# Unnormalised exponentials in the first four stages of an attention and feed-forward kernel, and float16 pairs for half of its first float32 units

## The chip, the cores and the metric

The kernel runs on one core of one Trainium2 chip. The metric is the device time of one execution in microseconds (us). The kernel before took 642.29 us (median of three runs: 640.42, 642.29 and 642.66).

## The reference

Attention over q, k and v of shape (4, 8, 768, 64), with a window of 16 around each query and 24 block summaries as extra keys, then a feed-forward layer on the 3072 tokens of 512 numbers (w_in is 512 x 2048, w_out 2048 x 512):

```python
k_sum = k.reshape(B, H, nb, block, D).max(axis=3)
v_sum = v.reshape(B, H, nb, block, D).mean(axis=3)
scores_l_m = np.where(np.abs(pos[:, None] - pos[None, :]) < window, scale * q @ k.T, -1e9)
scores_s = scale * np.einsum('bhsd,bhnd->bhsn', q, k_sum) + np.log(block)
scores_all = np.concatenate([scores_l_m, scores_s], axis=-1)
a = np.exp(scores_all - scores_all.max(axis=-1, keepdims=True))
a = a / (a.sum(axis=-1, keepdims=True) + 1e-09)
x = a @ np.concatenate([v, v_sum], axis=2)          # (token, head * 64 + d)
h = x @ w_in
out = (h * (1.0 / (1.0 + np.exp(-h)))) @ w_out
```

The weights arrive as float64, everything else as float32; the output is float32.

## The kernel before, in words

**Tiling.** Attention is cut into 24 stages of 128 queries (stage s is tile s mod 6 of batch s // 6), each of four jobs m = 4s + g of two heads. A query tile sees 158 local keys and 24 summaries, 182 columns. A job (`job_a`) computes its scores on PE (L587 in batch 0, in float32 on 64 rows of the array; L589 and L590 with split operands later) into a PSUM bank, takes the masked row maximum on DVE (L594), the exponential with its row sum on ACT (L597), and the sum's reciprocal on DVE (L602, L603). In a "plain" stage (s < NPL, before: stages 0 and 1) the exponentials are scaled by the reciprocal (L612 or L608), transposed on PE (L621, L623: a "turn") and copied back to SBUF in two halves; `job_c` multiplies them with float32 v at once (L653). In the other stages they are scaled into float16 p (L608, L610, L612), the rounding remainder is made on DVE (L636, four instructions for a job), a DMA transposes both (L639), and `job_c` multiplies with float16 pairs of v (L668, 40 matmuls for a stage). `job_x` takes the stage's result from bank 7 into the float16 pair xh, xl (L222 on ACT, L229 on DVE).

**Feed-forward.** Two stages make a chunk of 256 tokens; 12 chunks of 8 units (f = 0 to 7, 256 of the 2048 columns) are 96 units. A unit is 24 matmuls 128x256 of FFN1 (L781: xh and xl with the pair of w_in), a tanh on ACT (L795), the product on DVE (L796), and FFN2 (L790). Chunks 0 and 1 (c < NPW) use float32 in FFN2, 4 matmuls 128x512 that the trace shows as 8 records (4 for each half of the tokens); the others use a float16 pair of g and of w_out, 12 matmuls 128x512 (6 for each half). The order of the units is (chunk 0, f 0 to 3), (1, f 0 to 3), (1, f 4 to 7), (0, f 4 to 7), then chunk after chunk.

**Weights.** w arrives as float64 in 16 tiles of 1 MB, loaded by SP. ACT (L704, L700) and DVE (L702, L706) turn each into float32. w_in tiles are then reduced (L716), gathered on PE (L720, L721), and split into a pair (L222 on ACT, L229 on DVE). w_out tiles are summed on ACT (L714) and split only after one scale `kap` over all of them is known (`job_wo`).

**Order.** All engines run in program order. That order is written by a planner (class `Plan`) that knows a cost in ns for every step and a priority from the table `TUNE`; it also puts fills (L321, matmuls into bank 0 that compute nothing) on PE where it expects PE to wait before the first unit.

Of the kernel before, what the change touches and what calls it, by code (L numbers as in the profile page):

```python
# [9 lines left out]
F32 = mybir.dt.float32  # L10
# [4 lines left out]
AF = mybir.ActivationFunctionType  # L15
# [33 lines left out]
NPL = 2  # L49
# [158 lines left out]
def local_attn_ffn(ctx: ExitStack, tc: tile.TileContext, qkT, qF, qD, kF, kD, v, vR, w, out):  # L208
# [100 lines left out]
    e_t = ring(NE, [P, 2, NKEY], F32, "e")  # L309
    p_all = const.tile([P, NP * 2 * UW], F16, name="p")  # L310
# [4 lines left out]
    part_t = [const.tile([P, 2, DM], F32, name=f"part{i}") for i in range(NSUP - 2)]  # L315
# [251 lines left out]
    def job_a(m, prio):  # L567
# [9 lines left out]
        k = (2, 3, 4, 5)[m % 4] if m < 8 else sbank()  # L577
        sc = bank[k].rearrange("p (a b) -> p a b", a=2)
        n = m % NE
        tt, ttk = tt_of(m)  # L580
        et, mx, pt = e_t[n], mx_t[n], p_t[m % NP]
        pr = slice(g % 2 * 64, g % 2 * 64 + 64)
# [18 lines left out]
        unit_sum = 1.0 if s < NPL else 1.0 / PSC
        plan.op({"dve": 72}, lambda e: nc.vector.tensor_scalar(out=su, in0=su, scalar1=1e-9, scalar2=unit_sum, op0=ALU.add, op1=ALU.mult), w=sums, prio=prio)  # L602
        plan.op({"dve": 75}, lambda e: nc.vector.reciprocal(out=su, in_=su), w=sums, prio=prio)  # L603

        def scaled(e, out, i):
            by = su[:, i:i + 1]
            if e == "act":
                nc.scalar.activation(out=out, in_=et[:, i, :], func=AF.Copy, scale=by)  # L608
            elif e == "pool":
                nc.gpsimd.tensor_scalar(out=out, in0=et[:, i, :], scalar1=by, scalar2=0.0, op0=ALU.mult, op1=ALU.add)  # L610
            else:
                nc.vector.tensor_scalar(out=out, in0=et[:, i, :], scalar1=by, scalar2=None, op0=ALU.mult)  # L612
# [28 lines left out]
    def job_c(m, prio):  # L641
# [15 lines left out]
        if g < 3:  # L657
            return
# [300 lines left out]
```

## Time and profile before

| | us |
|---|---|
| median of three runs | 642.29 |
| profiled execution | 642.86 |
| its span in the profile | 641.1 |
| PE busy | 629.0 (98%) |
| DVE busy | 467.8 (73%) |
| ACT busy | 407.6 (64%) |
| POOL busy | 178.9 (28%) |
| first matmul of the first unit | 52.30 |
| first matmul of unit 8 | 105.16 |
| first matmul of unit 16 | 165.02 |

The profiled execution is 1.76 us longer than its span and 0.57 us above the median. A row of the trace gives a start, a duration, engine, line, operation, what is written and read, and how many alike instructions in a row it holds; PE's rows include the tail of the last matmul, so the next row can start before one ends. The chain of waits gives times from one start to the next instead.

### The profile page before, as it was taken

Reading aid. Unit: us, or ns where it says so; the run is one execution under the profiler, and the core shown is the slowest. Engines: PE = TensorE matmul, PEld = TensorE weight load, DVE = VectorE, ACT = ScalarE, POOL = GpSimd, SP = SyncE. Lnnn points to the kernel's source line nnn. Section 1 sums busy time; section 2 is a strip of 40 time slices with the busy share of each in tenths; the row PEclk is TensorE's granted clock in tenths of the full one; section 3 lists DMA queues with packets and bytes.
Section 4 is the critical chain, followed back from the end, with each engine's and each line's share of the span. In section 5 each row is a group of like instructions: output and inputs, shape, how many; then the busy total and the mean of one; then the engine's idle time right before and its main releaser. Section 6 shows DMA issues by size and latency. Waiting matters only on the chain.

```text
span 641.1 us, 13605 instructions
## 1 busy us (share of the span) xinstructions
PE 629.0 (98%) x4940; PEld 425.8 (66%) x4940; DVE 467.8 (73%) x1365; ACT 407.6 (64%) x895; POOL 178.9 (28%) x200
## 2 busy tenths in 40 slices
PE   7999999999999999999999999999999998999997
PEld 2667666656676776667677676666776675767664
DVE  6999886899779954897779855899898984231322
ACT  3899897964677655765778655656887863332322
POOL 3035232110564222242534245024542330000000
PEclk9999999999999999999999999999999999999999
DMA  8869986365485665665484774566686551000000
GB/s 308 308 195 304 295 341 179 98 192 138 131 191 122 135 187 194 144 170 137 122 198 121 175 225 127 141 174 118 196 179 153 113 129 32 35 0 1 34 1 33
DMA packets 99237, 97.37 MB, mean 152 GB/s; under 512 B 76886, under 2 KB 79958, under 8 KB 97122
## 3 DMA queue, kind: packets, MB, share of 16 engines
q1 hardware_dynamic: 99170, 96.51, 54.7%
q8 instruction: 38, 0.62, 0.4%
q14 instruction: 29, 0.24, 0.1%
HBM read 70.34 MB, written 6.29 MB: 120 GB/s over the span
## 4 chain that ended last, share of the span: by engine, by line
PE 65%; DVE 12%; ACT 8%; DMA 8%; issue 3%; SPq 2%; POOL 2%; POOLq 0%; DVEq 0%; ACTq 0%
PE bank L790 29%; PE bank L781 27%; DVE p L636 4%; DMA raw<-in_v_dram 2%; PE bank L668 2%; PE bank L587 2%; DVE qk L494 2%; DMA raw<-vms 2%; DMA raw<-in_kD_dram 2%; ACT wt L704 2%; DVE e L594 1%; PE bank L589 1%; PE bank L590 1%; PE bank L522 1%; DMA wt<-in_w_dram 1%
## 5 line engine op out<-in xcount | busy, mean ns | idle before, releaser
L790 PE MATMUL bank<-wt,g 128*128 128x512 f16 (+1 forms) x1088 | 283.2, 405 | 3.1 <-ACT g L800 1.1
L781 PE MATMUL bank<-xh,wt 128*128 128x256 f16 x1536 | 269.6, 273 | 0.0
L781 PEld LDWEIGHTS <-wt 128*128 128x128 f16 x2304 | 224.1, 98 | 43.0 <-issue 5.0
L781 PE MATMUL bank<-xl,wt 128*128 128x256 f16 x768 | 209.3, 273 | 0.0
L790 PEld LDWEIGHTS <-g 128*128 128x128 f16 x960 | 91.9, 98 | 96.2 <-DVE g L232 1.6
L796 DVE SCALAR_TENSOR_TENSOR t<-t,bank 128x512 f32<-128x512 f32 x96 | 65.6, 683 | 75.6 <-ACT t L795 75.2
L795 ACT ACTIVATE t<-bank,asc 128x512 f32<-128x512 f32 x96 | 65.2, 680 | 74.0 <-PE bank L781 73.5
L597 ACT ACTIVATE e<-e,mx 128x182 f32<-128x182 f32 x192 | 83.9, 439 | 35.9 <-DVE mx L594 32.9
L636 DVE SCALAR_TENSOR_TENSOR p<-e,sum,p 128x128 f16<-128x128 f32 x352 | 100.9, 349 | 7.9 <-ACT p L608 5.8
L232 POOL TENSOR_TENSOR g<-t,g 128x512 f16<-128x512 f32 x41 | 53.0, 1293 | 101.8 <-ACT g L800 101.7
L610 POOL TENSOR_SCALAR p<-e,sum 128x182 f16<-128x182 f32 x72 | 40.4, 567 | 142.1 <-DVE sum L603 42.1
L800 ACT CAST g<-t 128x512 f16<-128x512 f32 x80 | 49.2, 615 | 41.6 <-DVE t L796 40.4
L594 DVE CUSTOM_DVE_ANT_0 e<-bank,masks,qsc 128x182 f32<-128x182 f32 x144 | 52.7, 401 | 12.4 <-PE bank L590 12.1
L232 DVE TENSOR_TENSOR g<-t,g 128x512 f16<-128x512 f32 x39 | 32.8, 840 | 21.2 <-ACT g L800 21.1
L608 ACT ACTIVATE p<-e,sum 128x182 f16<-128x182 f32 x89 | 36.4, 439 | 13.8 <-DVE sum L603 5.2
L232 POOL TENSOR_TENSOR vv<-raw,vv 128x1024 f16<-128x1024 f32 x18 | 40.4, 2247 | 8.0 <-ACT vv L214 4.9
L790 PEld LDWEIGHTS bank<-wt,g 128*128 128x128 f32 x128 | 22.5, 190 | 23.2 <-issue 20.3
L597 ACT ACTIVATION_READ_ACCUMULATOR e<-e,mx 128x1 f32 x192 | 36.3, 189 | 0.0
L494 DVE SCALAR_TENSOR_TENSOR qk<-raw,qsc,qk 64x1264 f16<-64x1264 f32 x18 | 28.9, 1608 | 1.6 <-ACT qk L493 1.0
L668 PEld LDWEIGHTS <-vv 128*64 128x64 f16 x880 | 25.2, 110 | 6.8 <-issue 6.4
L493 ACT ACTIVATE qk<-raw,qsc 128x1264 f16<-128x1264 f32 x18 | 24.2, 1344 | 6.9 <-DMA raw<-in_kD_dram 6.9
L589 PE MATMUL bank<-qk 128*128 128x182 f16 x144 | 27.7, 242 | 0.0
(153 smaller groups left out, 656.3 us busy)
## 6 DMA issues: line engine op xcount, KB each, us to landing
wt<-in_w_dram SPq DMA_DIRECT2D x16, 1024.0 KB
raw<-in_kD_dram SPq DMA_DIRECT2D x18, 632.0 KB
raw<-in_v_dram SPq DMA_DIRECT2D x20, 512.0 KB
raw<-in_qD_dram SPq DMA_DIRECT2D x18, 512.0 KB
out_dram<-raw SPq DMA_DIRECT2D x24, 256.0 KB
raw<-in_kF_dram SPq DMA_DIRECT2D x12, 384.0 KB
raw<-in_qF_dram SPq DMA_DIRECT2D x9, 512.0 KB
raw<-in_vR_dram SPq DMA_DIRECT2D x12, 384.0 KB
```

Source lines behind the costliest of these rows:

```text
L232: eng[e].tensor_tensor(out=out, in0=in0, in1=in1, op=ALU.subtract)
L494: plan.op({"dve": 1450}, lambda e: nc.vector.scalar_tensor_tensor(out=kst[64:, :, :NLOC], in0=kr[64:], scalar=qs[64:, 1:2], in1=kst[64:, : ...
L594: plan.op({"dve": 258 if b == 0 else 323}, lambda e, i=i: nc.vector.tensor_tensor_reduce(out=et[:, i, :], in0=sc[:, i, :NKEY], in1=mask, s ...
L597: plan.op({"act": 431}, lambda e, i=i, h=h: nc.scalar.activation(out=et[:, i, :], in_=et[:, i, :], func=AF.Exp, scale=-1.0, bias=mx[:, i:i ...
L610: nc.gpsimd.tensor_scalar(out=out, in0=et[:, i, :], scalar1=by, scalar2=0.0, op0=ALU.mult, op1=ALU.add)
L636: nc.vector.scalar_tensor_tensor(out=pt[:, i, to:to + z - a], in0=et[:, i, a:z], scalar=su[:, i:i + 1], in1=pt[:, i, a:z], op0=ALU.mult, o ...
L668: nc.tensor.matmul(out=av[j * D:(j + 1) * D, i * P:(i + 1) * P], lhsT=vt[:, vi, h * D:(h + 1) * D], rhs=tt[:, j * 3 + blk, :], start=(n == ...
L781: nc.tensor.matmul(out=h[:, d * CH:(d + 1) * CH], lhsT=wt[f, 0][:, part, d, ct * P:(ct + 1) * P], rhs=x[:, ct, :], start=(ct == 0 and q == ...
L790: nc.tensor.matmul(out=bank[ob[u]], lhsT=a[:, d * CH + u * P:d * CH + u * P + P], rhs=b[:, d, :], start=(opens and d == 0 and q == 0), sto ...
L795: plan.op({"act": 640}, lambda e: nc.scalar.activation(out=t, in_=h, func=AF.Tanh, scale=asc_t[c // 3 % 2][:, f:f + 1]), r=[("bank", k), ( ...
L796: plan.op({"dve": 605}, lambda e: nc.vector.scalar_tensor_tensor(out=t, in0=t, scalar=1.0, in1=h, op0=ALU.add, op1=ALU.mult), r=[("bank", ...
L800: plan.op({"act": 540}, lambda e: nc.scalar.copy(out=gh, in_=t), r=[("t", j)], w=[("gh", n)], prio=at - TUNE["post"])
```

## The change: what it does

- `NPL` goes from 2 to 4: stages 0 to 3 are plain. In them the exponentials are not scaled. Their sums are collected in a tile `ss` of 128x8 for a stage; `job_x` inverts it, spreads it over 64 rows with eight float32 matmuls (`over`, L691 of the new kernel) into bank 1, 1, 5 or 4, scales that (`xr`), multiplies bank 7 with it on DVE (L695), casts to xh on ACT (L697) and makes xl on POOL or DVE.
- In batch 0 the scores of two jobs are issued together, alternating between rows 0 to 63 and 64 to 127 of the array and between banks k and k + 1.
- A turn is copied back at once, 512 columns, instead of in two halves; banks 2 to 5 are cleared at the start for that.
- The product with v of a plain stage is issued once a stage, 16 matmuls (L657), and not once a job.
- Units f = 4 to 7 of chunks 0 and 1 use the float16 pair in FFN2. Their banks close after f = 3, the partial result is scaled and kept, and is added at the end. So `kap` and the first pairs of w_out are needed by unit 8 instead of unit 16.
- All numbers of `TUNE` are other ones, and with them the order on every engine; some costs of the planner too.

```diff
-NPL = 2
+NPL = 4
+    for i in range(2, 6):
+        nc.vector.memset(bank[i], 0.0)
...
-        k = (2, 3, 4, 5)[m % 4] if m < 8 else sbank()
+        k = (2, 3, 4, 5)[m % 4] if m < 8 else (4, 5)[m % 2] if m < 16 else (6, 7)[m % 2] if b == 0 else sbank()
...
-                    nc.tensor.matmul(out=sc[:, i, :NKEY], lhsT=qk[pr, hp, :P], rhs=qk[pr, hp, P:], start=True, stop=True)
+                    for o in range(2):
+                        pr = slice(o * 64, o * 64 + 64)
+                        nc.tensor.matmul(out=bank[k + o][:, i * 256:i * 256 + NKEY], lhsT=qk[pr, hp, :P], rhs=qk[pr, hp, P:], start=True, stop=True)
...
-                out=et[:, i, :], in_=et[:, i, :], func=AF.Exp, scale=-1.0, bias=mx[:, i:i + 1], accum_out=su[:, i:i + 1]),
+                out=et[:, i, :NKEY], in_=et[:, i, :NKEY], func=AF.Exp, scale=-1.0, bias=mx[:, i:i + 1], accum_out=ss_t[s % 2][:, 2 * g + i:2 * g + i + 1] if plain else su[:, i:i + 1]),
...
-            for i in range(2):
-                plan.op({"dve": 190, "act": 310}, lambda e, i=i: scaled(e, et[:, i, :], i), r=sums, w=[("e", n, i)], prio=prio)
...
-            plan.op({"act": 264, "dve": 335}, lambda e: copy(e, tt[:, :2, :], tp[:, :2, :]), r=[("bank", k)], w=[ttk], prio=prio, port=())
-            plan.op({"act": 264, "dve": 335}, lambda e: copy(e, tt[:NS2, 2:, :], tp[:NS2, 2:, :]), r=[("bank", k)], w=[ttk + ("side",)], prio=prio, port=())
+            plan.op({"act": 530, "dve": 600}, lambda e: copy(e, tt, tp), r=[("bank", k)], w=[ttk], prio=prio, port=())
...
+            rb = (1, 1, 5, 4)[s]
+            def over(e):
+                for h in range(H):
+                    g, j = divmod(h, 2)
+                    nc.tensor.matmul(out=bank[rb][j * D:(j + 1) * D, g * P:(g + 1) * P], lhsT=ss[:, h:h + 1].to_broadcast([P, D]), rhs=ident, start=True, stop=True)
+            plan.op({"act": 600, "dve": 600}, lambda e: times(e, xr, bank[rb], vsc_t[0][:, 0:1]), r=[("bank", rb), ("vsc", 0)], w=[("xr", s % 2)], prio=prio, port=())
+            plan.op({"dve": 620}, lambda e: nc.vector.tensor_tensor(out=xr, in0=bank[k], in1=xr, op=ALU.mult), r=[("bank", k)], w=[("xr", s % 2)], prio=prio, port=())
+            plan.op({"act": 560}, lambda e: nc.scalar.copy(out=xh, in_=xr3), r=[("xr", s % 2)], w=[("xh", z, half)], prio=prio)
+            plan.op({"dve": 680, "pool": 1280}, lambda e: less(e, xl, xr3, xh), r=[("xr", s % 2), ("xh", z, half)], w=[("xl", z, half)], prio=prio)
...
-        plain = c < NPW
+        plain = c < NPW and f < QF
-        split = c < NSUP - 2
+        split = c < NSUP
...
-    job_wo(need_c[NPW] - TUNE["kap"])
+    job_wo(need_f[QF] - TUNE["kap"])
```

**PE ahead of the first unit.** In the kernel before, all sixteen jobs' scores and the whole of stages 0 and 1 stand ahead of the first L781 (bank_195 is bank 0, bank_201 bank 6, bank_202 bank 7); the last rows ahead of it, and the first row of it:

```order
L587 MATMUL bank_201<-qk_152 128x182 x2
...
L653 MATMUL bank_202<-wt 64x128 x4
L587 MATMUL bank_201<-qk_152 128x182 x2
L653 MATMUL bank_202<-wt 64x128 x12
L587 MATMUL bank_201<-qk_152 128x182 x2
...
L720 MATMUL bank_201<-wm,spread 128x2
L721 MATMUL bank_201<-least,spread 128x2
...
L668 MATMUL bank_202<-wt,vv_166 64x128
...
L781 MATMUL bank_195<-xh_186,wt 128x256
```

In the new kernel (bank_199 is bank 0, bank_206 bank 7), lines 591, 611 and 613, 657, 691 and 801 are scores, turns, the product with v, `over` and FFN1:

```order
L591 MATMUL bank_203<-qk_152 128x182
L591 MATMUL bank_204<-qk_152 128x182
...
L691 MATMUL bank_200<-ident,ss_177 64x128 x8
L657 MATMUL bank_206<-wt 64x128 x16
L611 MATMUL bank_203<-ident,e_174 128x128 x2
L613 MATMUL bank_203<-ident,e_174 54x128 x2
...
L691 MATMUL bank_200<-ident,ss_178 64x128 x8
L657 MATMUL bank_206<-wt 64x128 x16
...
L801 MATMUL bank_199<-xh_190,wt 128x256
```

Of stages 2 and 3 only one joint score pair and one turn stand ahead of the first unit now; the float16 product L668 that stood there has gone, and 61 fills stand ahead of the first L801 instead of 105.

**PE between units 1 and 3 of the new kernel** (bank_203 and bank_204 are banks 4 and 5; L810 is FFN2):

```order
L810 MATMUL bank_201<-wt,g_196 128x512 x2
L691 MATMUL bank_204<-ident,ss_177 64x128 x8
L810 MATMUL bank_202<-wt,g_196 128x512 x2
...
L591 MATMUL bank_203<-qk_152 128x182
L591 MATMUL bank_204<-qk_152 128x182
...
L657 MATMUL bank_206<-wt 64x128 x16
L611 MATMUL bank_203<-ident,e_174 128x128 x2
```

In the kernel before, PE had at that place, beside L781 and L790, only the gathers and one L668 product. Seven turns, three score pairs, two `over` and two products with v, fourteen pieces of stages 2 and 3, now stand from unit 0 to ahead of unit 4.

**DVE ahead of the first unit.** Before, remainders of p and the operand xl of chunk 0:

```order
L636 SCALAR_TENSOR_TENSOR p<-e_174,sum_168,p 128x128
L636 SCALAR_TENSOR_TENSOR p<-e_174,sum_168,p 128x54
...
L716 TENSOR_REDUCE wm<-wt 128x1
...
L229 SCALAR_TENSOR_TENSOR xl_188<-bank_202,vsc_164,xh_186 128x4x128
```

Now (L736 is L716 of before, L684, L685 and L695 are new, L599 is L594 of before):

```order
L599 ISA e_175,mx_172<-bank_204,masks 128x182
...
L736 TENSOR_REDUCE wm<-wt 128x1
L695 TENSOR_TENSOR xr_179<-bank_206,xr_179 128x512
L684 TENSOR_SCALAR ss_178<-ss_178 128x8
...
L685 RECIPROCAL ss_178<-ss_178 128x8
...
L226 TENSOR_SCALAR xr_180<-bank_200,vsc_164 128x512
...
L695 TENSOR_TENSOR xr_180<-bank_206,xr_180 128x512
```

The twenty remainders are gone, and the operand's last step before ACT's cast is a product on DVE.

## Rows read from the trace of the kernel before

**Rows 1.** Windows: start:end, us, then busy us (instructions) of PE, PEld, DVE, ACT, POOL; clock, DMA share, GB/s.

```profile
11.20:49.30 38.10, 38.06 (x263) 24.58 (x262) 36.29 (x151) 33.08 (x99) 6.62 (x11) 1.00 0.83 265
52.30:105.20 52.90, 52.22 (x318) 33.13 (x315) 45.85 (x67) 47.89 (x67) 18.40 (x17) 1.00 0.86 294
105.20:165.00 59.80, 59.80 (x386) 38.00 (x385) 49.56 (x146) 41.06 (x85) 9.55 (x14) 1.00 0.52 145
```

**Rows 2.** Chain of waits, 145 to 167 and 560 to 570: start, us, what.

```profile
147.87 1.24 PE bank L668 x40
149.11 1.91 PE bank L790 x4
...
153.29 1.72 PE bank L790 x4
155.01 2.62 PE bank L781 x24
...
563.17 5.18 PE bank L790 x24
```

**Rows 3.** Chain of waits, start-up, PE.

```profile
9.56 1.52 PE bank L587 x8
11.08 1.53 PE bank L522 x2
...
14.25 0.97 PE bank L522 x2
15.22 0.81 PE bank L587 x4
...
17.00 0.37 PE bank L621 x2
17.37 0.22 PE bank L623 x2
```

**Rows 4.** Timeline of PE: start, us, instruction.

```profile
33.44 1.54 PE L653 MATMUL bank<-wt 128*64 128x128 f32 x16
```

**Rows 5.** DVE, 11.2 to 49.3, by form: count, busy us, mean ns, idle before.

```profile
L594 DVE CUSTOM_DVE_ANT_0 e<-bank,masks 128x182 f32<-128x182 f32 x32 | 10.0, 339 | 1.5 <-PE bank L587 1.5
L706 DVE SCALAR_TENSOR_TENSOR wt<-wt 128x1024 uint32<-128x1024 uint32 x4 | 4.9, 1217 | 0.1
L716 DVE TENSOR_REDUCE wm<-wt 128x1 f32<-128x1024 f32 x4 | 4.8, 1208 | 0.0
L636 DVE SCALAR_TENSOR_TENSOR p<-e,sum,p 128x128 f16<-128x128 f32 x10 | 3.6, 360 | 0.4 <-POOL p L610 0.4
L636 DVE SCALAR_TENSOR_TENSOR p<-e,sum,p 128x54 f16<-128x54 f32 x10 | 2.7, 265 | 0.0
L594 DVE DVE_READ_ACCUMULATOR2_ANT mx<- 128x1 f32 x32 | 2.6, 81 | 0.1
L612 DVE TENSOR_SCALAR e<-e,sum 128x182 f32<-128x182 f32 x9 | 2.5, 313 | 0.0
L602 DVE TENSOR_SCALAR sum<-sum 128x2 f32<-128x2 f32 x13 | 2.0, 156 | 0.0
...
L363 DVE TENSOR_REDUCE km<-wt 128x24 f32<-128x768 f32 x2 | 1.9, 950 | 0.0
L229 DVE SCALAR_TENSOR_TENSOR xl<-bank,vsc,xh 128x512 f16<-128x512 f32 x2 | 1.5, 736 | 0.0
```

**Rows 6.** ACT, the same stretch and columns.

```profile
L597 ACT ACTIVATE e<-e,mx 128x182 f32<-128x182 f32 x32 | 14.0, 441 | 6.2 <-DVE mx L594 4.9 <-DVE sum L603 0.9
```

**Rows 7.** Timeline of POOL, then DVE, around 50 us.

```profile
47.96 2.13 POOL L232 TENSOR_TENSOR vv<-wt,vv 128x1024 f16<-128x1024 f32 x1
...
49.49 1.69 DVE L229 SCALAR_TENSOR_TENSOR wt<-wt,ur 128x1024 f16<-128x1024 f32 x1
...
53.55 1.28 DVE L229 SCALAR_TENSOR_TENSOR wt<-wt,ur 128x1024 f16<-128x1024 f32 x1
```

**Rows 8.** Timeline of DVE: the last decoding of a weight tile.

```profile
95.31 1.97 DVE L706 SCALAR_TENSOR_TENSOR wt<-wt 128x1024 uint32<-128x1024 uint32 x1
```

More of the change, by code (lines that the diff above doesn't have):

```diff
@@ L590, in scores @@
                     nc.tensor.matmul(out=sc[:, i, :NKEY], lhsT=ql[:, h, :], rhs=kst[:, h, :], start=False, stop=True)
-        plan.op({"pe": 640 if b == 0 else 330}, scores, r=[(x, s % 2, hp) for x in ("qk", "qkm") for hp, _ in heads(g)] + [("qkk", s % 2)], w=[("bank", k)], prio=prio, cols=728)
+        if b or g % 2 == 0:
+            plan.op({"pe": 330 if b else 820}, scores, r=[(x, s % 2, hp) for x in ("qk", "qkm") for hp, _ in heads(g)] + [("qkk", s % 2)], w=[("bank", k)] if b else [("bank", k), ("bank", k + 1)], prio=prio, cols=728)
@@ L600, in job_a @@
+                w=[("e", n, i), ("ss", s % 2, 2 * g + i) if plain else ("sum", m % 3, i)], prio=prio)
         er, sums = [("e", n, 0), ("e", n, 1)], [("sum", m % 3, 0), ("sum", m % 3, 1)]
[L601 to L612, printed above, removed]
@@ L644, in job_c @@
         av = bank[7]
+        if g < 3:
+            return
         if s < NPL:
-            tt, ttk = tt_of(m)
             vr, key = plain_v[s]
+            parts = [tt_of(4 * s + i) for i in range(4)]
             def direct(e):
                 for blk in range(2):
-                    for j in range(2):
-                        rows = slice(0, P if blk == 0 else NS2)
-                        nc.tensor.matmul(out=av[j * D:(j + 1) * D, g * P:(g + 1) * P], lhsT=vr[rows, blk, (2 * g + j) * D:(2 * g + j + 1) * D], rhs=tt[rows, 2 * blk + j, :], start=(blk == 0), stop=(blk == 1))
-            plan.op({"pe": 850}, direct, r=[ttk, ttk + ("side",)] + key, w=[("bank", 7)], prio=prio, cols=728)
-            return
-        if g < 3:
+                    rows = slice(0, NS2 if blk else P)
+                    for i, (tt, _) in enumerate(parts):
+                        for j in range(2):
+                            nc.tensor.matmul(out=av[j * D:(j + 1) * D, i * P:(i + 1) * P], lhsT=vr[rows, blk, (2 * i + j) * D:(2 * i + j + 1) * D], rhs=tt[rows, 2 * blk + j, :], start=(blk == 0 and i == 0), stop=(blk == 1 and i == 3))
+            plan.op({"pe": 2100}, direct, r=[ttk for _, ttk in parts] + key, w=[("bank", 7)], prio=prio, cols=2912)
             return
@@ L808, in job_f @@
             src = bank[ob[u]]
+            pt = plain_w[c, 0][:, u, :] if split else None
             if f < NFP - 1:
-                pt = part_t[c][:, u, :]
-                plan.op({"act": 478, "dve": 598}, lambda e, pt=pt, src=src: copy(e, pt, src), r=[("bank", ob[u])], w=[("part", c, u)], prio=at - TUNE["post"])
+                plan.op({"act": 600, "dve": 600}, lambda e, pt=pt, src=src: times(e, pt, src, vsc_t[c // 3 % 2][:, 1:2]), r=[("bank", ob[u]), ("vsc", c // 3 % 2)], w=[("wv", c, 0)] if u == 0 else [("part", c)], prio=at - TUNE["post"], port=())
                 continue
@@ L839, in job_stage @@
             job_km(b, p[0] - TUNE["km"])
[L840 removed]
+        if s == NPL:
             for i in range(NP):
@@ L886, in local_attn_ffn @@
     plan.issue()
-TUNE = dict(wo=446.0, kap=120.96, km=193.98, w_dma=118.35, w_dec=-99.08, a0=174.58, a1=-468.24, d1=455.82, span=3.23, post=200.49, ffn2=-434.13, jc0=1039.26, jc1=-3.66, jx0=275.52, jx1=-673.16, vs=1070.72, qk=-145.44, k=-197.61, v=228.96, v0=83.48, out=338.89, first=69.59)
+TUNE = dict(wo=1435.66, kap=595.44, km=324.46, w_dma=-292.18, w_dec=-36.51, a0=618.19, a1=-173.71, d1=488.76, span=-168.31, post=-84.22, ffn2=-1333.64, jc0=2019.41, jc1=670.33, jx0=530.16, jx1=21.06, vs=2765.61, qk=-268.51, k=382.38, v=2035.94, v0=-52.65, out=942.25, first=210.86)
 NUDGE = {}
```

44 lines of the change are left out of this document (29 added, 15 removed).

## The prediction

> **What bounds the kernel now.** I read the windows first. From the first unit to the end PE is busy in nearly all of the time: 52.22 of 52.90 us in units 0 to 7, 59.80 of 59.80 in units 8 to 15 [rows 1]. There a us taken out of PE's queue is a us of time. Behind 165 us it is the same but for small gaps. The first 52.3 us are another matter: PE is full there too, but of fills, which take no part in the result. What sets the first unit is when its last operand, xl of chunk 0, leaves DVE. So I read DVE and ACT from the first score reduction (11.2) to that operand (49.3): DVE is busy in 36.29 of 38.10 us, ACT in 33.08 [rows 1]. DVE bounds that stretch, with ACT close behind: ACT's exponentials idle 6.2 us, 4.9 of them for DVE's maxima [rows 6].
>
> So three sums: the time of the first unit (52.3 before), from there to unit 16 (112.7 before: 52.90 + 59.80) [rows 1], and the rest (641.1 − 165.0 = 476.1).
>
> **Until the first unit.** DVE's groups of that stretch [rows 5], with fourteen smaller ones, add to 45.8 us. The engine is busy 36.29 because records overlap, so a group costs .79 of its busy sum. What leaves the stretch, read from the new order:
> - half of the 32 score reductions and of their accumulator reads, since stages 2 and 3 come later: 5.0 + 1.3;
> - all twenty remainders of p: 3.6 + 2.7;
> - nine scalings of exponentials: 2.5;
> - 22 of the 26 small sums and reciprocals (13 of each, alike): 3.4;
> - three of four weight reductions and two of four decodings, which move behind the first unit: 3.6 + 2.5;
> - the two key reductions, now ahead of the first scores, and the two operands xl from the bank, replaced below: 1.9 + 1.5.
>
> That is 28.0 us by busy sums, 22.1 of the engine's time. What enters: turns copied 512 wide (1.2 more for the halves that they replace, an estimate from the 512-wide xl at .74, [rows 5]), two products with bank 7 and one scaling of `xr` (at .66 each, .74 less the overlap, 2.0), one weight split moved forward (1.3 by [rows 7]), the two sums of `ss` (.3): 4.8. So 38.1 − 22.1 + 4.8 = 20.8. The first scores start about 11.9, as one key load now stands behind four loads of v on SP's queue (.7 later than 11.2). That gives 32.7; the cast on ACT and the remainder on POOL come behind it, 1.9 (half of POOL's 2.13 for half of its columns, [rows 7], and .8 for the cast, between .44 for 182 columns and three times that, [rows 6]): 34.6. I add 1.4 for waits between the engines, much less than ACT's 6.2 of before as DVE holds less that it waits for: the first unit starts at **36**. Without waits it is 33. If PE's start-up loses as much over its real work as before (10.7 us), it is 41. Of what leaves, remainders, scalings and small sums are never done again; the rest is done behind the first unit, under PE's work.
>
> **From unit 0 to unit 16, PE.** Start to start, one FFN1 takes 2.62, half a float32 FFN2 1.72 (1.91 behind a float16 product), a float16 FFN2 half of 5.18 [rows 2]:
> - 16 FFN1: 42.0.
> - 8 float32 FFN2 at 3.55 (two halves between 1.72 and 1.91): 28.4. Before, 15.5 of them took 55.0.
> - 7 float16 FFN2 at 2.59: 18.1. A unit is dearer in float32 by .96, so the eight changed ones give 7.7.
> - 7 joint score pairs. The single score of a job took .81; the first two jobs, issued next to one another on both halves of the array, 1.52 [rows 3]. That was with the array still slow: two matmuls L522 took 1.53 right behind, and .97 at 14.25 [rows 3], and the trace's first clock record (1.00) is at 12.2. I take half of 1.52, .76, for a pair, against two singles, 1.62: 5.3.
> - 7 turns at .59 [rows 3], less overlap: 3.7.
> - two `over`: eight matmuls 64 rows wide are as many records as sixteen of L653, 1.54 [rows 4]: 3.1. Two products with v of a whole stage, 32 records or twice 1.54 less overlap, 2.94 [rows 4]: 5.9.
> - two float16 products (stages 4 and 5) at 1.24 [rows 2]: 2.5; gathers and small matmuls: 2.8.
>
> Sum: 111.8. The same sum for before gives 110.3 against the measured 112.7, so 2.4 us are not in it (waits, and switches between shapes). I add these 2.4, and 3 for new waits between 0 and 5: PE now runs the fourteen pieces of stages 2 and 3 between units, and scores of stages 4 and 5 share bank 7 with the product with v. That is 117.2: **unit 16 starts at 153** instead of 165.0. Can DVE and ACT follow? DVE's busy time up to unit 16 falls by the remainders, scalings and sums of stages 2 and 3, but must be done by 153: before, 49.56 of 59.80 us went by in units 8 to 15 [rows 1]; by the new order I count 49 us of work in 52.6 there. It fits, barely, which is why I keep the waits.
>
> **From unit 16 to the end.** Nothing of the change is here but what slips behind: a float16 unit in place of a float32 one as the last leftover FFN2, and two more jobs' scores, +1.5. 476.1 + 1.5 = 477.6. Other edits cost nothing visible: the four memsets on DVE stand ahead of the first scores, where DVE waits for loads; the partial result's scaling and final addition run on ACT and DVE under FFN1, where DVE is idle 13 to 17% of the time and ACT 9 to 31% [rows 1]; if that cover were gone each costs about .7 us once for four banks.
>
> **Sum.** 36 + 117.2 + 477.6 = 630.8 of span, and 1.76 beside the span as in the profiled execution: 632.6, say **632.5**. The profiled execution (642.86) is .57 above the median, which the rounding of my terms covers.
>
> **One rule against it.** The remainder xl of stages 0 to 3 goes to POOL now, four times, with DVE at weight splits beside it. In the trace the split that met a POOL subtraction took 1.69 instead of 1.28, with .60 us of overlap [rows 7]: .41 each, 1.6 for four, inside my 3 us of waits.
> The Trainium skill (SBUF — State Buffer, "SBUF: two separate sides") says that the pair of ports which DVE with two SBUF inputs shares with GpSimd is an exclusive lock, so that the later one waits for the whole instruction. The trace agrees in kind: the split ended late by two thirds of the overlap. By that rule the four would cost DVE up to four whole POOL subtractions, some 4.3 by half of the POOL row's 2.13, and the sum would be 635 where DVE has no slack.
>
> **The rivals.**
> - *The scale comes late* (15 in 100). FFN2 of unit 8 now waits for `kap`, and so for the last decoded weight tile; DVE finished that one at 97.3 [rows 8], and kap, the first split and its signals took some 5 more at their shortest. If the last load is no earlier than before, FFN2 of unit 8 can start at 102.8 where PE wants it at 100.4: +2.4, 635. Loads fill 86% of the DMA engines' time up to there [rows 1], which speaks for it; that the planner has to do them for unit 8 and starts the units 16 us earlier speaks for both. Each us later costs one: up to 642.
> - *Stages 2 and 3 stall PE between units* (11 in 100, the slower side). PE's queue is in order: a turn that is not ready holds FFN1 behind it. A pair needs, from its first matmul, .76, a reduction of .26 and two exponentials of .44 before its first turn, about 2.2 with signals, and about .9 more for its second; the order leaves one FFN1 (2.62) or less. One weight step of 1.2 to 1.3 on DVE or ACT ahead of it [rows 5, 7] uses the slack up and more. With one such step in front of each of the fourteen pieces, 14 × 1.2 = 16.8 in place of my 3: 646.3, slower. It decides at 1.15 us a piece. Against: in units 0 to 7 of before PE waited under 1 us though weights were decoded there all the time. With half of it: 638.
> - *The halves of the array do not run beside one another* (4 in 100). Then a pair costs 1.62: +.86 × 7 = 6, 638.6.
> - *The clock falls* (4 in 100). It was at its upper level (1.00) in every stretch from 12.2 us on [rows 1], with fills ahead of the first unit and PE never idle; the change takes 44 fills out, and puts waits between units. One unit at the lower level costs its own 6.2 again: 638.8, two 645. The Trainium skill (TensorE: Matmul & The Clock Gate, Part 1) says that an idle array falls back to half of its clock; no row of before shows it behind 12.2 us.
> - *It goes better* (5 in 100): first unit at 33, no new waits: 625 or less.
>
> **How the numbers follow.** The forecast (625 to 637) has the remaining 61 in 100. A measurement of this kernel tells about 0.5% from no change, 3.2 us: faster is under 639.1, slower over 645.5. Faster takes the forecast, the good case, two thirds of the late scale (10), and half of the array and clock cases (3): 79. Slower takes most of the stalls: 9. The rest, 12, lies between. The range from 624 to 642 leaves out the stalls (10), the second half of the clock case (2) and the far end of the good case (3).
>
> **What would show it.** First unit at 33 to 41; unit 8 about 52 us behind it, unit 16 at 150 to 158; eight FFN2 less in float32 (64 records); joint scores at .76 a pair of jobs; no remainders of p before stage 4; PE's idle time between 36 and 153 under 6 us. Wrong: a wait of PE ahead of the first FFN2 of unit 8 of more than 3 us (the scale), waits ahead of turns that add up to over 8 us (the stalls), a granted clock under 1.00 behind 15 us, or a first unit behind 41, with DVE or ACT full until there.

## The result, and the profile after

The changed kernel took 631.67 us (median of four runs, 631.11 to 633.1) against 642.19 for the kernel before: a ratio of .9845, 95% interval .982 to .987, faster by 1.6%. The forecast was 632.5, range 624 to 642. The table has the stretches of the profiled execution, as differences of starts that are rounded to .1 us.

| us | before | forecast | after |
|---|---|---|---|
| first unit starts | 52.3 | 36 | 35.4 |
| unit 0 to unit 16 | 112.7 | 117.2 | 113.7 |
| unit 16 to the end | 476.1 | 477.6 | 481.0 |
| span | 641.1 | 630.8 | 630.1 |

The windows of the changed kernel (same columns as [rows 1]): the stretch up to chunk 0's last operand, units 0 to 7 and 8 to 15, where PE's queue is full, and the rest.

```profile
11.20:33.00 21.80, 21.70 (x213) 15.50 (x212) 18.61 (x66) 17.33 (x46) 1.79 (x3) 1.00 0.98 357
35.40:92.20 56.80, 56.76 (x415) 39.61 (x413) 48.65 (x84) 55.65 (x93) 15.14 (x15) 1.00 0.68 248
92.20:149.10 56.90, 54.70 (x417) 35.03 (x416) 51.68 (x137) 39.34 (x83) 12.53 (x17) 1.00 0.52 140
149.10:630.10 481.00, 471.32 (x3926) 326.77 (x3924) 339.94 (x1000) 280.61 (x629) 150.44 (x157) 1.00 0.51 126
```

Ahead of the first unit DVE has 18.61 us of work where it had 36.29 [rows 1]; PE stays full behind it, at clock 1.00. ACT is at 55.65 of 56.80 in units 0 to 7, which I had not foreseen. DVE's groups in that first stretch answer to [rows 5]: the remainders are gone, 19 score reductions are left of 32, one weight reduction of four.

```profile
L599 DVE CUSTOM_DVE_ANT_0 e<-bank,masks 128x182 f32<-128x182 f32 x19 | 5.6, 333 | 2.3 <-PE bank L591 1.9 <-ACT e L602 0.4
...
L726 DVE SCALAR_TENSOR_TENSOR wt<-wt 128x1024 uint32<-128x1024 uint32 x2 | 2.4, 1209 | 0.0
...
L736 DVE TENSOR_REDUCE wm<-wt 128x1 f32<-128x1024 f32 x1 | 1.2, 1202 | 0.0
```

PE's timeline answers to [rows 3, 4]: a joint score pair (L591), `over` (L691), a stage's product with v (L657), and the records of two turns (L611, L613).

```profile
16.61 0.89 PE L591 MATMUL bank<-qk 64*128 64x182 f32 x8
...
22.76 1.09 PE L691 MATMUL bank<-ident,ss 128*64 128x128 f32 x16
23.69 2.06 PE L657 MATMUL bank<-wt 128*64 128x128 f32 x32
...
42.33 0.42 PE L611 MATMUL bank<-ident,e 128*128 128x128 f32 x2
42.58 0.38 PE L613 MATMUL bank<-ident,e 128*54 128x128 f32 x2
42.80 0.38 PE L611 MATMUL bank<-ident,e 128*128 128x128 f32 x2
43.02 0.38 PE L613 MATMUL bank<-ident,e 128*54 128x128 f32 x2
```

From one start to the next, two jobs' scores take about .82 us (I had .76), `over` .9 to 1.0 (1.54), a product with v 2.0 (2.94), a turn .47 (.53).

### The profile page after: what moved, and what is told of

It reads as the page before. It is cut to its first block, busy times and chain, and to the rows that moved or that the text cites. A ratio compares the mean times of both kernels' runs of the same rounds, so it can differ in the third digit from the quotient of the medians.

```text
span 630.1 us, 13616 instructions
## 1 busy us (share of the span) xinstructions
PE 614.5 (98%) x5008; PEld 422.3 (67%) x5008; DVE 470.2 (75%) x1317; ACT 397.2 (63%) x860; POOL 186.0 (30%) x213
## 5 line engine op out<-in xcount | busy, mean ns | idle before, releaser
L810 PE MATMUL bank<-wt,g 128*128 128x512 f16 (+1 forms) x1120 | 276.9, 392 | 4.7 <-POOL g L232 3.2
L801 PE MATMUL bank<-xh,wt 128*128 128x256 f16 x1536 | 269.8, 273 | 1.0 <-DVE raw L835 0.9
L801 PEld LDWEIGHTS <-wt 128*128 128x128 f16 x2304 | 224.3, 98 | 46.5 <-issue 6.5
L801 PE MATMUL bank<-xl,wt 128*128 128x256 f16 x768 | 209.3, 273 | 1.4 <-DVE xl L229 1.4
L810 PEld LDWEIGHTS <-g 128*128 128x128 f16 x1056 | 100.6, 98 | 107.5 <-POOL g L232 6.7
L232 POOL TENSOR_TENSOR g<-t,g 128x512 f16<-128x512 f32 x56 | 72.4, 1292 | 152.6 <-ACT g L820 134.4
L637 DVE SCALAR_TENSOR_TENSOR p<-e,sum,p 128x128 f16<-128x128 f32 x320 | 89.7, 343 | 3.3 <-ACT p L624 2.4
L820 ACT CAST g<-t 128x512 f16<-128x512 f32 x88 | 54.0, 614 | 34.0 <-DVE t L816 33.5
L599 DVE CUSTOM_DVE_ANT_0 e<-bank,masks,qsc 128x182 f32<-128x182 f32 x144 | 52.1, 401 | 8.4 <-PE bank L594 8.1
L626 POOL TENSOR_SCALAR p<-e,sum 128x182 f16<-128x182 f32 x62 | 28.6, 470 | 99.4 <-ACT e L602 36.2
L624 ACT ACTIVATE p<-e,sum 128x182 f16<-128x182 f32 x75 | 30.3, 439 | 22.7 <-DVE sum L619 8.5
L232 POOL TENSOR_TENSOR vv<-raw,vv 128x1024 f16<-128x1024 f32 x17 | 37.5, 2206 | 14.8 <-ACT vv L214 10.9
L593 PE MATMUL bank<-qk 128*128 128x182 f16 x144 | 27.8, 242 | 0.0
L594 PE MATMUL bank<-qk 128*128 128x182 f16 x144 | 27.8, 242 | 0.0
L670 PE MATMUL bank<-tt,vv 128*64 128x128 f16 x800 | 26.1, 220 | 0.0
```

The costliest lines, as they stand in the source:

```text
L232: eng[e].tensor_tensor(out=out, in0=in0, in1=in1, op=ALU.subtract)
L637: nc.vector.scalar_tensor_tensor(out=pt[:, i, to:to + z - a], in0=et[:, i, a:z], scalar=su[:, i:i + 1], in1=pt[:, i, a:z], op0=ALU.mult, o ...
L670: nc.tensor.matmul(out=av[j * D:(j + 1) * D, i * P:(i + 1) * P], lhsT=vt[:, vi, h * D:(h + 1) * D], rhs=tt[:, j * 3 + blk, :], start=(n == ...
L801: nc.tensor.matmul(out=h[:, d * CH:(d + 1) * CH], lhsT=wt[f, 0][:, part, d, ct * P:(ct + 1) * P], rhs=x[:, ct, :], start=(ct == 0 and q == ...
L810: nc.tensor.matmul(out=bank[ob[u]], lhsT=a[:, d * CH + u * P:d * CH + u * P + P], rhs=b[:, d, :], start=(opens and d == 0 and q == 0), sto ...
L820: plan.op({"act": 540}, lambda e: nc.scalar.copy(out=gh, in_=t), r=[("t", j)], w=[("gh", n)], prio=at - TUNE["post"])
```

## The experiments

Every run's stretches, from the first FFN1 matmul of units 0 and 16 and the end of the span, as differences of rounded starts. They are those of the one profiled execution: the slowest of its kernel in new_numbers_only (674.05) and direct_by_job (638.41), the fastest in gl_640 (639.75). The ratio is to the kernel before on the same chip (there 641.0 to 641.4 us); the two load runs have one time each.

| kernel | median us | ratio (95%) | first unit | 0 to 16 | 16 to end |
|---|---|---|---|---|---|
| before | 642.19 | 1 | 52.3 | 112.7 | 476.1 |
| changed | 631.67 | .9845 (.982 to .987) | 35.4 | 113.7 | 481.0 |
| undo_pairs | 649.05 | 1.012 (1.006 to 1.018) | 35.7 | 130.3 | 481.0 |
| only_pairs | 655.22 | 1.019 (1.013 to 1.025) | 55.1 | 112.8 | 486.4 |
| old_numbers | 643.09 | 1.003 (.998 to 1.007) | 48.3 | 110.7 | 481.4 |
| new_numbers_only | 668.35 | 1.041 (1.033 to 1.048) | 62.5 | 119.2 | 490.5 |
| two_plain | 648.58 | 1.011 (1.006 to 1.015) | 51.4 | 117.9 | 476.9 |
| serial_halves | 629.69 | .981 (.977 to .986) | 34.2 | 113.8 | 478.2 |
| direct_by_job | 635.44 | .990 (.987 to .994) | 37.5 | 115.2 | 483.7 |
| gl_640 | 642.02 | 1.001 (.998 to 1.004) | 33.9 | 120.3 | 483.7 |
| after_again | 629.59 | .982 (.977 to .988) | 35.7 | 113.8 | 478.3 |
| dve_load | 633.98 | | 41.0 | 113.7 | 477.5 |
| act_load | 638.14 | | 43.2 | 113.8 | 479.1 |
| gl_dve | 641.64 | 1.002 (.999 to 1.005) | 35.4 | 124.7 | 479.4 |

### Do the parts add? undo_pairs and only_pairs

Float32 back in the changed kernel, or the pairs alone in the kernel before (each with the lines for closing the banks, scaling the output and the splits' due times that belong to it):

```diff
-        plain = c < NPW and f < QF
+        plain = c < NPW
...
-        split = c < NSUP
+        split = False
...
-    job_wo(need_f[QF] - TUNE["kap"])
+    job_wo(need_c[NPW] - TUNE["kap"])
```

> The changed kernel with float32 again in FFN2 of all units of chunks 0 and 1, their banks open until the end as before, and the scale over w_out due at unit 16 again; stages 0 to 3 and the table of numbers stay as changed. Theory (parts add up on PE's queue): 8 units at 3.55 us instead of 2.59 us give +7.7 us, so unit 16 starts 7 to 8 us later than 149.1 (156 to 157) and the time is 639 to 640 us. Rival A (the earlier scale and the earlier splits of w_out cost DVE and ACT about what PE saves): the time stays within 2 us of 631.7. Rival B (the order is tuned for the pairs): more than 643 us.

```diff
-        plain = c < NPW
+        plain = c < NPW and f < QF
...
-        split = c < NSUP - 2
+        split = c < NSUP
...
-    job_wo(need_c[NPW] - TUNE["kap"])
+    job_wo(need_f[QF] - TUNE["kap"])
```

> The kernel before with nothing but the float16 pairs of units f = 4 to 7 of chunks 0 and 1 (banks closed after f = 3, scale over w_out due at unit 8), with the numbers of before. Theory: first unit at 52.3 as before, units 0 to 16 shorter by up to 7.7 us, less what the earlier scale makes PE wait at unit 8 (DVE is busy in 45.85 of the 52.90 us ahead of it): 635 to 639 us. Rival A (scale late, DVE full with the remainders of stages 2 and 3): no gain, 640 to 646 us. Rival B (nothing hinders it): 634 us or less.

Neither came out as my theory had it. Undoing the pairs cost 16.6 us between units 0 and 16, not 7.7. FFN2 took 57.5 us there (start to start) against 49.1. But these are sixteen units against fifteen, as this order puts one more FFN2 ahead of unit 16: a float32 unit took 3.6 us and a float16 one, with its waits, 3.0, so eight changed units make 4.7, and the one more 3.6. Of the other 8.1, 4.8 are added waits of PE (start to start, a wait counts to the record ahead of it), and 2.2 are scores of batch 1, which in the changed kernel come behind unit 16. The windows of undo_pairs, units 8 to 12 and 12 to 16:

```profile
96.90:127.00 30.10, 30.10 (x157) 17.93 (x156) 12.46 (x33) 18.43 (x33) 1.00 (x3) 1.00 0.29 92
127.00:166.00 39.00, 33.76 (x258) 21.20 (x257) 36.77 (x124) 26.53 (x63) 7.25 (x14) 1.00 0.64 167
```

In the first DVE works 12.46 of 30.10 us, in the second 36.77 of 39.00 while PE has gaps: work for which there was room in the first is put where it is wanted at once. Pairs alone gave the kernel before nothing: units 0 to 16 stayed at 112.8, as FFN2 took 3.8 us less but attention 4.0 more, which this order puts inside them. The other stretches grew by 2.8 and 10.3; in the first of them the clock stood at .50 from 47.5 to 54.3. Rival B of undo_pairs and rival A of only_pairs are nearest; only_pairs came out slower still.

### Is it the table of numbers? old_numbers and new_numbers_only

The line `TUNE` exchanged, nothing else; for new_numbers_only the same the other way round in the kernel before.

```diff
-TUNE = dict(wo=1435.66, kap=595.44, km=324.46, w_dma=-292.18, w_dec=-36.51, a0=618.19, a1=-173.71, d1=488.76, span=-168.31, post=-84.22, ffn2=-1333.64, jc0=2019.41, jc1=670.33, jx0=530.16, jx1=21.06, vs=2765.61, qk=-268.51, k=382.38, v=2035.94, v0=-52.65, out=942.25, first=210.86)
+TUNE = dict(wo=446.0, kap=120.96, km=193.98, w_dma=118.35, w_dec=-99.08, a0=174.58, a1=-468.24, d1=455.82, span=3.23, post=200.49, ffn2=-434.13, jc0=1039.26, jc1=-3.66, jx0=275.52, jx1=-673.16, vs=1070.72, qk=-145.44, k=-197.61, v=228.96, v0=83.48, out=338.89, first=69.59)
```

> The changed kernel with the table of numbers of before, everything else as changed. Theory (the parts carry the gain, the table only places them): the first unit starts at 35 to 42 us because remainders and scalings of stages 2 and 3 are gone from DVE whatever the order, total 632 to 640 us. Rival (the gain is the new table's): the first unit stays behind 46 us and the time within 2 us of 642 or above.

> The kernel before with the table of numbers of the changed kernel, nothing else. Theory (parts carry the gain): no gain, 640 to 660 us, as DVE has the same work ahead of the first unit, which starts at 48 us or later unless stages 2 and 3 are put behind it, where their remainders then hold up PE. Rival (the table carries it): 637 us or less.

With the old numbers the first unit comes at 48.3, not at 35 to 42, and the time is that of before. DVE's groups of old_numbers from 11.2 to 47 say why:

```profile
L726 DVE SCALAR_TENSOR_TENSOR wt<-wt 128x1024 uint32<-128x1024 uint32 x6 | 7.3, 1224 | 0.2 <-ACT wt L724 0.2
L736 DVE TENSOR_REDUCE wm<-wt 128x1 f32<-128x1024 f32 x6 | 7.3, 1216 | 0.0
```

Six weight tiles are decoded and six reduced ahead of the first unit: 14.6 us, against 3.6 in the changed kernel. The two starts are 12.9 us apart. Of these, 3.4 pass ahead of the first score reduction (16.98 against 13.54), where this order has the scale of v and one decoding; the other 9.5 are behind it, with DVE busy in 33.55 of the 35.80 us of that window. The new numbers alone are worse still, 62.5 and 668: the order that they write goes with the parts. So neither the parts nor the numbers carry the gain by themselves. What a table made for each variant would give was not tried.

### Do stages 2 and 3 have to be plain? two_plain

```diff
-NPL = 4
+NPL = 2
```

> The changed kernel with NPL = 2: stages 2 and 3 again as before with float16 p, remainders and DMA transposes, all else of the change (unnormalised exponentials in stages 0 and 1, joint scores, pairs, numbers) kept. PE has 7 us less to do between unit 0 and unit 16 (no turns, no over, 1.24 instead of 2.05 us for a product with v), DVE some 8 to 10 us more beside 100 of 113.7 us. Theory (DVE bounds there, that is why stages 2 and 3 became plain): 640 to 650 us, the loss between units 0 and 16. Rival (PE bounds even so): 626 to 631 us.

As the theory said, in total (648.58). But mostly not in the place that it named: 16.0 us of the loss are in the first unit (51.4) and only 4.2 between units 0 and 16. PE had some 7 us less to do there, and waited 10.1 us instead of 2.2, so the theory's mechanism is there, as the smaller part. DVE's groups of two_plain from 11.2 to 49 show five weight reductions and six decodings ahead of the first unit again, 13.3 us:

```profile
L726 DVE SCALAR_TENSOR_TENSOR wt<-wt 128x1024 uint32<-128x1024 uint32 x6 | 7.3, 1216 | 0.0
L736 DVE TENSOR_REDUCE wm<-wt 128x1 f32<-128x1024 f32 x5 | 6.0, 1208 | 0.0
```

### Two prices on PE: serial_halves and direct_by_job

```diff
-            for i, (hp, h) in enumerate(heads(g)):
-                if b == 0:
-                    for o in range(2):
-                        pr = slice(o * 64, o * 64 + 64)
+            for o in range(2 if b == 0 else 0):
+                pr = slice(o * 64, o * 64 + 64)
+                for i, (hp, h) in enumerate(heads(g)):
...
```

> The changed kernel with the eight records of a joint score pair in another order: both heads of the job on rows 0 to 63 first, then both of the job on rows 64 to 127, as the first two jobs stood in the kernel before; nothing else moves. Theory A (the halves run beside one another only where their matmuls alternate): a pair takes 1.62 us instead of 0.82, seven pairs from unit 0 to unit 16 give +5.6 us, and the time is 636 to 638 us. Theory B (each half has its own queue, and order does not matter within eight records): 0.8 to 0.9 us a pair and 631 to 633 us.

Theory B holds: the pair takes the same with the halves one after the other in the queue (timeline of serial_halves). So my reading of the first pair of before was right, and alternating is not what makes it fast.

```profile
20.74 0.89 PE L590 MATMUL bank<-qk 64*128 64x182 f32 x8
```

```diff
-                for blk in range(2):
-                    rows = slice(0, NS2 if blk else P)
-                    for i, (tt, _) in enumerate(parts):
+                for i, (tt, _) in enumerate(parts):
+                    for blk in range(2):
+                        rows = slice(0, NS2 if blk else P)
...
-                            nc.tensor.matmul(out=av[j * D:(j + 1) * D, i * P:(i + 1) * P], lhsT=vr[rows, blk, (2 * i + j) * D:(2 * i + j + 1) * D], rhs=tt[rows, 2 * blk + j, :], start=(blk == 0 and i == 0), stop=(blk == 1 and i == 3))
+                            nc.tensor.matmul(out=av[j * D:(j + 1) * D, i * P:(i + 1) * P], lhsT=vr[rows, blk, (2 * i + j) * D:(2 * i + j + 1) * D], rhs=tt[rows, 2 * blk + j, :], start=(blk == 0), stop=(blk == 1))
```

> The changed kernel with the product with v of a plain stage in the order of the kernel before: per job 128 rows for two heads, then 54 rows for two heads, instead of all 128-row matmuls first; nothing else moves. In the changed kernel 32 records take 2.0 us, before 32 took about 2.9. Theory (it is the change between 128 and 54 rows that costs): 2.8 to 3.0 us again for a stage, two stages between unit 0 and unit 16 give +1.8, two ahead of the first unit up to +1.8 more if they are on its path: 633 to 635 us. Rival (the 2.0 us come of the longer run of matmuls, whatever its order): 2.0 to 2.2 us, 631 to 633.

The theory holds: a stage's product takes 2.95 to the next start again (timeline of direct_by_job), +1.8 us of L657 between units 0 and 16 and +1.8 ahead of unit 0, where the start moved by 2.1 (by 1.5 when counted from the first score reduction). The edit moves more than the order: the start and stop flags are again given for each job, as before, and the run does not tell the two apart.

```profile
54.12 3.01 PE L657 MATMUL bank<-wt 128*64 128x128 f32 x32
```

### One cost of the planner: gl_640

```diff
-            plan.op({"pool": 1280, "dve": 690}, lambda e: less(e, gl, t, gh), r=[("t", j), ("gh", n)], w=[("gl", n)], prio=at - TUNE["post"])
+            plan.op({"pool": 1280, "dve": 640}, lambda e: less(e, gl, t, gh), r=[("t", j), ("gh", n)], w=[("gl", n)], prio=at - TUNE["post"])
```

> The changed kernel with one cost of the planner put back: the remainder of g is charged 640 ns on DVE as before, not 690, so that fewer of them go to POOL (56 of 88 in the changed kernel, 41 of 80 before). The part from unit 16 to the end took 481.0 us, 3.4 more than forecast. Theory (remainders on POOL come late and hold FFN2): that part shrinks by 1 to 3 us, 628 to 631 us. Rival (the waits come of the table's order of attention): it stays within 1 us of 481 or grows, 631 us or more.

The rival holds, and far beyond what it said: 50 ns in one cost wrote another order and took the whole gain away, 6.6 us of it between units 0 and 16. PE stands there for the transposed p of a stage and for the scale of batch 1, which DVE had not made (timeline of gl_640):

```profile
151.42 0.47 PE L670 MATMUL bank<-tt,vv 128*64 128x128 f16 x10 [1.21 <-DMA tt<-p]
...
153.59 0.34 PE L593 MATMUL bank<-qk 128*128 128x182 f16 x1 [1.39 <-DVE vsc L438]
```

The window from the end of the second wait on:

```profile
153.20:156.60 3.40, 3.01 (x16) 2.23 (x17) 1.86 (x8) 0.75 (x1) 0.31 (x1) 0.50 0.44 112
```

The clock (the third number from the end) fell to .50 there, behind the wait of 1.21 us and within that of 1.39. PE's waits between units 0 and 16 are 4.8 us in all, against 2.2 in the changed kernel.

### What sets the first unit: dve_load and act_load

Results of the added instructions are not used; after_again is the base on this chip. The first two added lines are those of dve_load, the others those of act_load.

```diff
+        for _ in range(6):
+            nc.vector.tensor_reduce(out=padt, in_=flat, axis=AX.X, op=ALU.max)
...
+        for _ in range(7):
+            nc.scalar.activation(out=padt, in_=flat, func=AF.Copy, scale=1.0)
```

> The changed kernel once more, as the base for the three others on this chip: 630 to 633 us, first unit at 34 to 36 us.

> The changed kernel with six reductions of 128x512 on DVE (about .68 us each, 4.0 us in all, results unused) ahead of the score reduction of job 4; order otherwise as changed. Theory (DVE's queue sets the first unit): the first unit starts 3.3 to 4.1 us later, at 38 to 39.5. Rival (chain of dependencies, loads or ACT): 0 to 1.5 us later, as DVE idles 3.2 of the 21.8 us from 11.2 to 33.0.

> The changed kernel with seven copies of 128x512 on ACT (about .58 us each, 4.0 us in all, results unused) ahead of the first exponential of job 4; order otherwise as changed. Theory (DVE sets the first unit, ACT idles 4.5 of 21.8 us there): 0 to 2 us later. Rival (both engines are links of one chain, whichever is loaded): 3 us or more later, as much as with the load on DVE.

DVE's load (six reductions) lasted 4.27 and moved the first unit from 35.7 to 41.0, by 5.3; ACT's lasted 4.59 and moved it to 43.2, by 7.5. That difference is mostly one of the start: the first score reduction stands well ahead of the loads, and it came 1.2 us earlier in dve_load than in after_again (DVE's timelines of after_again, dve_load and act_load):

```profile
13.89 0.35 DVE L599 CUSTOM_DVE_ANT_0 e<-bank,masks 128x182 f32<-128x182 f32 x1 [1.20 <-PE bank L591]
...
12.71 0.34 DVE L606 CUSTOM_DVE_ANT_0 e<-bank,masks 128x182 f32<-128x182 f32 x1
...
14.05 0.35 DVE L606 CUSTOM_DVE_ANT_0 e<-bank,masks 128x182 f32<-128x182 f32 x1 [1.47 <-PE bank L598]
```

Counted from it, the first unit comes after 21.8, 28.3 and 29.2 us: 6.5 later with the load on DVE, 7.4 with that on ACT. So my theory fell for ACT, and the rival holds: in the changed kernel the start is one chain through PE, DVE and ACT with little slack in any. And both moved it by more than they lasted. PE's timelines of dve_load and, last, act_load show a turn waiting for the late exponentials, and what comes behind it in dve_load taking longer than in the changed kernel:

```profile
23.09 0.91 PE L618 MATMUL bank<-ident,e 128*128 128x128 f32 x2 [3.51 <-ACT e L609]
...
25.41 1.59 PE L598 MATMUL bank<-qk 64*128 64x182 f32 x8
26.93 1.97 PE L698 MATMUL bank<-ident,ss 128*64 128x128 f32 x16
...
25.23 0.91 PE L618 MATMUL bank<-ident,e 128*128 128x128 f32 x2 [4.15 <-ACT e L609]
```

The windows of dve_load give the reason in their clock column (the third number from the end):

```profile
20.00:22.00 2.00, 0.00 (x0) 0.00 (x0) 1.90 (x4) 0.00 (x0) 0.00 (x0) 1.00 0.93 389
...
24.00:26.00 2.00, 2.00 (x10) 1.22 (x10) 1.97 (x8) 1.86 (x5) 0.00 (x0) 0.50 1.12 448
26.00:28.00 2.00, 2.00 (x18) 1.59 (x16) 1.84 (x8) 0.00 (x0) 0.00 (x0) 0.50 1.05 397
```

PE idled 3.51 us, and ran at the lower level (.50, 1.2 GHz) until about 30 us; the score pair and `over` took 1.59 and 1.97 instead of .89 and 1.09. From the start of that pair to the next turn it is 5.9 us instead of 3.7: these 2.2 and the 4.27 make the 6.5. In act_load the clock stood at .50 from 25.5 to 32.4, behind the wait of 4.15. In the changed kernel no wait of that length stands there, and the clock stays at 1.00 from 12 us on.

### POOL beside DVE: gl_dve

```diff
-            plan.op({"pool": 1280, "dve": 690}, lambda e: less(e, gl, t, gh), r=[("t", j), ("gh", n)], w=[("gl", n)], prio=at - TUNE["post"])
+            plan.op({"dve": 690}, lambda e: less(e, gl, t, gh), r=[("t", j), ("gh", n)], w=[("gl", n)], prio=at - TUNE["post"])
```

> The changed kernel with all remainders of g on DVE, none on POOL (56 of 88 were there). In the changed kernel DVE instructions that met a POOL subtraction lasted until it was over (a remainder of p took 1.28 instead of .34 us at 111.96, POOL's subtraction ran from 111.94 to 113.09); over the whole kernel such stretched instructions add some 40 us to DVE. Theory A (the port is held for a whole POOL instruction, so POOL's help costs DVE as much as it saves): DVE's busy time from unit 16 to the end rises by less than 15 us though it gets 45 more remainders of .66, and the time stays within 4 us of the changed kernel. Theory B (POOL's help is free): DVE busy rises by 30 us or more in that part and the time by over 5 us. The planner writes another order for this kernel, which alone can cost some us.

From unit 16 on DVE took over 48 remainders of g (80 instead of 32), 33 us by .69 each; its busy time there rose by 14.9 us, 355.35 against 340.47 in after_again. Each remainder became shorter (DVE's groups of that part, of after_again with the scalings of the output, then of gl_dve):

```profile
L232 DVE TENSOR_TENSOR g<-t,g 128x512 f16<-128x512 f32 x32 | 29.9, 933 | 14.4 <-ACT g L820 13.3 <-issue 0.8
...
L226 DVE TENSOR_SCALAR raw<-bank,osc 128x512 f32<-128x512 f32 x7 | 5.2, 748 | 0.7 <-PE bank L810 0.7
```

```profile
L232 DVE TENSOR_TENSOR g<-t,g 128x512 f16<-128x512 f32 x80 | 59.9, 749 | 18.3 <-ACT g L820 17.9
```

The 14.9 is just within theory A's 15, but it does not show theory A, as the rest of DVE's work is not the same: the seven scalings of the output are on ACT in gl_dve, and six score reductions and some splits of that part now come ahead of unit 16. What the remainders themselves give back is 32 times .933 - .749, 5.9 us. Over the whole kernel, DVE's instructions that lasted more than .15 us over the median of their kind add 32.5 us in after_again, not the 40 that I named, and 26.7 in gl_dve. By both counts POOL's remainders of g cost DVE some 6 us, a small part of the 33 that they save it.

That part did not get longer (479.4 against 478.3). The time did, by 12 us and so beyond theory A's 4, nearly all of it between units 0 and 16 (124.7): another order, as in gl_640. PE waited 7.5 us there instead of 2.2, and from 140.9 to 147.7 the clock stood at .50, from within a wait of 3.16 us on, with two of .83 and .58 ahead of it (window of gl_dve):

```profile
140.90:147.70 6.80, 4.74 (x16) 2.16 (x17) 6.51 (x18) 2.33 (x4) 0.82 (x2) 0.50 0.73 244
```

Whether a table made for this variant would be faster was not tried.

## Why the prediction was right, point by point

The total is off by .8 us, and that is closer than its terms are: the start was .6 lower than forecast, units 0 to 16 3.5 lower, the rest 3.4 higher. The mechanism of each stretch stands as below; that their errors cancel is luck.

- **First unit, 36 against 35.4.** Right as a sum, with two terms off that offset one another, which is luck too. The first score reduction came at 13.54 and not at 11.9: PE does eight records of the means of v ahead of the first scores, and the clock stood at .50 from 7.6 to 11.1 meanwhile. In serial_halves, where it was 1.00 from 6.3 on, the same eight took 3.66 us instead of 5.29 and the reduction came at 12.55. The stretch from it to the last operand (DVE's L695, ended 32.44) took 18.9 and not 20.8. Behind that, the last xl ended on POOL at 34.33, and the 1.0 us left are two gathers and a turn that stand ahead of unit 0 in PE's queue. The reason that I gave, DVE bounds, was half of it: work taken from DVE was what had to go (old_numbers, with 14.6 us of weight work there instead of 3.6, starts at 48.3), but once it was gone, a load on ACT moved the start as much as one on DVE.
- **Unit 0 to 16, 117.2 against 113.7.** Mis-sized terms: products with v 4.1 and not 5.9, `over` 2.0 and not 3.1, turns 3.4 and not 3.7, score pairs 5.7 and not 5.3. I had taken prices per record from a row that changes between 128 and 54 rows of the array after every four records; direct_by_job gives .9 us a stage for that, the flags included. FFN1 (42.5), float32 FFN2 (28.1) and the float16 products (2.5) were as forecast. Of 5.4 us for switches and waits, 4.6 are found: 3.0 in float16 FFN2 (2.0 of them waits), 1.6 in small matmuls; the waits that the trace names there are 2.2 us in all.
- **Unit 16 to the end, 477.6 against 481.0.** Low by 3.4, and by .7 against the repeat (478.3). In the profiled execution PE waited 2.2 us there for remainders of g on POOL and 1.4 for ACT's cast, against .6 and 1.1 before: waits that I had not carried into that part. All its waits there make 5.9 us, against 3.5 before; in the repeat they make 3.3, so most of the excess belongs to that one execution and not to the kernel.
- **The scale late:** did not happen. The last decoding ended at 86.4 (97.3 before, [rows 8]) and kap was written at 102.6; the order gives PE sixteen records of postponed float32 FFN2 from 94.85 to 101.8 meanwhile.
- **Stalls in stages 2 and 3:** none of the fourteen pieces shows a wait between units 0 and 4. The order is what prevents it; in gl_640, gl_dve and undo_pairs PE's waits between units 0 and 16 came to 4.8, 7.5 and 5.6 us instead of 2.2, most of them at units 12 to 16, many ahead of the scores and means of batch 1. They are a part of the 6.6, 11.0 and 16.6 us by which that stretch grew. So a record that is not ready and holds up PE's queue was a real danger, at another place than I had put it.
- **Halves of the array:** they run beside one another (.82 for two jobs), in either order.
- **The clock:** 1.00 from 12 us to unit 16 and behind it. But the rival's mechanism is there in other orders: 6.8 us at the lower level in dve_load, behind a wait of 3.51 us, 6.8 in gl_dve and 3.4 in gl_640, at the waits named above. What the lower level cost in gl_640 and gl_dve was not measured by itself.
- **The rule on the shared port:** the trace bears it out better than the row that I weighed. The Trainium skill (SBUF — State Buffer, "SBUF: two separate sides") has the later one wait for the whole instruction; here DVE's L722 took 1.41 instead of .69, and ended .55 behind POOL's end (the page also counts DVE's 2-port modes; L722 reads one tensor, and no trace here shows its mode). Two of the four xl on POOL, and what they met on DVE, in the timelines of the changed kernel:

```profile
65.67 1.22 DVE L726 SCALAR_TENSOR_TENSOR wt<-wt 128x1024 uint32<-128x1024 uint32 x1
...
66.11 1.79 POOL L232 TENSOR_TENSOR xl<-xr,xh 128x512 f16<-128x512 f32 x1 [4.78 <-ACT xh L697]
...
69.47 1.17 POOL L232 TENSOR_TENSOR xl<-xr,xh 128x512 f16<-128x512 f32 x1 [1.03 <-ACT xh L697]
...
69.78 1.41 DVE L722 TENSOR_SCALAR wt<-wt 128x1024 uint32<-128x1024 uint32 x1
```

Three of the four xl met such an instruction. Where POOL's started second, POOL paid: 1.79 us beside L726, and 1.31 beside a weight split at 31.56, instead of 1.16. Only at 69.47 did DVE pay, .72 us, not the 4.3 of the rule for all four.

What I did not forecast is that the sum only holds for this order. I added the parts as if each kept its worth; the pairs or stages 2 and 3 taken back alone, with the planner free to write a new order, cost some 17 us of the time each (the pairs' own price was 7.7), and the old table took back all of the gain.

## What to carry to other kernels

Where engines run in program order and one of them is full, a change that takes work from the others is worth what the order makes of it: cost the parts from rows, but read the new order before believing the sum, and measure a part only together with the order made for it. In a start-up that is a chain through several engines, removing work from the busiest one makes the others the next link at once. Group matmuls of one row count, and look at the clock behind PE's waits: in dve_load a wait of 3.51 us cost its length and then 2.2 us more at .50. Before reading a shift of one us or two in a start-up, look at where its first work stands: with the same order ahead of it, the first score reduction came between 12.55 (serial_halves) and 14.05 (act_load).

## What the runs showed of the hardware that was not expected

- Changing between 128 and 54 rows after every four float32 records instead of once, with start and stop flags for each job, cost .9 us in 32 records (2.95 against 2.0).
- Records of float32 scores on rows 0 to 63 and on 64 to 127 overlap without alternating in the queue: eight in about .82, where four on one half take .81 [rows 3].
- The clock went to .50 behind waits of PE of 3.51 us (dve_load) and 4.15 (act_load), and in gl_640 behind one of 1.21 and within one of 1.39. Six reductions of 4.27 us on DVE moved the first unit by 6.5 us, seven copies of 4.59 us on ACT by 7.4, counted from the first score reduction.
- A POOL subtraction of 128x512 that started during a DVE decoding took 1.79 us instead of 1.16 (66.11); a DVE shift that started during such a subtraction took 1.41 instead of .69 (69.78). Whichever came second was the longer one.
- The same kernel in another set of runs differed by 2 us in its median (631.67 and 629.59), and its two profiled spans by 2.2, nearly all of it in float16 FFN2 behind unit 16 (214.7 and 212.5 us start to start), and of that 1.9 in waits.
